# Moving two chunks of weight conversion from the MLP to the experts, and squaring from SBUF instead of PSUM

## The chip, the cores and the metric

The kernel runs on one core of a Trainium2 chip. The metric is the device time of one execution in microseconds (us), here the median of three runs. One more execution was recorded by the profiler; all rows of the trace come from that one.

## The reference

Three stages run one after the other on 3072 tokens of width 256. The first is a chunked linear attention. The second is a mixture of experts in which every token goes to one of eight. The third is an MLP whose hidden layer is squared after the relu:

```python
def _moe_ref(x, w_gate, w1, w2):
    ...
        h = np.maximum(xe @ w1[e], 0.0)
        ye = h @ w2[e]
...
def _moe2_ref(x, w_in, w_out):
    h = x @ w_in              # 256 -> 2048
    r = np.maximum(h, 0.0)
    g = r * r
    return (g @ w_out).astype(np.float32)   # 2048 -> 256
```

## The kernel before, in words

Every float32 product is made from parts that TensorE takes at its fast rate: an operand is split into a high part (rounded to fp32r) and a low part (what is left), and three products are summed (high by high, high by low, low by high).

**Experts** (`Moe.run`). The work is a written-out list of 72 steps: 16 for the most used expert, which is cut into two parts, and eight for each of the other seven, whose columns shrink from 440 to 360. A step n does `up` for one slice of 128 hidden units (six matmuls into one PSUM bank `h`, of which there are two; ScalarE makes the high part `hh`, VectorE the low part `hl`) and then `down` for the slice of two steps earlier (six matmuls). The counter w = n - 8 sets everything else. Expert weights come in four pieces an expert, `wst` (two loads of 256 KB each, L153 and L155, issued by SyncE), with three buffers; piece w//2+7 is loaded in each odd step, ScalarE makes its high part `whi` (L161) four steps after the load was issued, VectorE its low part `wlo` (L168) in two halves.

**Conversion of the MLP's weights** (`Wide`). The MLP's two weight matrices arrive as 64-bit floats in 16 chunks of 512 KB (`wide.load`, L199 and L202, tile `w64`, two buffers). `Wide.step` turns a chunk into a high and a low part in three steps: i=0 is one ScalarE instruction (L222) and three of VectorE (L223 to L225), i=1 one of ScalarE (L228) and two of VectorE (L227, L229), i=2 two of VectorE (L231, L232). Chunks 0 to EARLY_W - 1 are converted inside the experts' steps, from the steps in the list `starts`; a chunk's third step also issues the load of the chunk two further on. The other chunks are converted inside the MLP, three to one step before they are needed (the table `conv` in `Mlp.run`).

**MLP** (`Mlp.run`). Tokens are cut into seven tiles: tile 0 and the last one have 256, the others 512. The steps are again a list: five slices of tile 0 (n = 0 to 4), then in turn one slice of tiles 1, 2 and 0, and from step 48 on one tile after the other. Step n does, in this order on each queue: what `conv` holds for n, then `up`, then the `down` of step n-3. `up` is six matmuls into a bank `h` (L983; three banks), then ScalarE `r` = relu (L987), VectorE `q` = square (L988), ScalarE `ga` = high part (L989), VectorE `gb` = low part (L990). `down` is six matmuls (L1005) for a slice of tile 0 and twelve for one of 512 tokens; the third of them is the first that reads `gb`. Each engine works through its own queue in order, so on ScalarE the `r` of the next step stands behind the `ga` of this one, and on VectorE the next `q` behind this `gb`. A third of the steps (tile 2) also carry one small instruction of a table (`rest_table`). At slice 8 of tiles 2 to 5 the next tile's input is split, its low part by GpSimd (`zl`, L969).

The lines that matter are these:

```python
steps += [(e, 2, f) for e in range(1, NE) for f in range(8)]     # Moe.run
starts = [6 + 52 * c // EARLY_W for c in range(EARLY_W)]
...
if w in (1, 4):
    wide.load(w // 4)
...
nc.scalar.activation(r, ps, ACTF.Relu)                           # Mlp.up
nc.vector.scalar_tensor_tensor(q, ps, 0.0, r, ALU.max, ALU.mult)
nc.scalar.activation(a, q, ACTF.Copy)
nc.vector.tensor_tensor(b, q, a.bitcast(F32), ALU.subtract)
```

Of the kernel before, what the change touches and what calls it, by code (L numbers as in the profile page):

```python
# [16 lines left out]
ALU = mybir.AluOpType  # L17
# [14 lines left out]

FILL = 512

EARLY_W = 10

AHEAD = 5
REG = 3584
# [85 lines left out]
class Ring:  # L124
# [45 lines left out]
    def up(self, part, e, f, kd):  # L170
        t = part[(4 * e + f // 2) % len(part)]
        o = kd * 256 + (f % 2) * 128
        return t[:, o:o + 128]
# [558 lines left out]
class Moe:  # L732
# [153 lines left out]
    def run(self, after):  # L886

        k = self.k
        ring, wide, v = k.ring, k.wide, k.nc.vector
        steps = [(0, 0, f) for f in range(8)] + [(0, 1, f) for f in range(8)]  # L890
        steps += [(e, 2, f) for e in range(1, NE) for f in range(8)]
        starts = [6 + 52 * c // EARLY_W for c in range(EARLY_W)]

        nz = (T - CAP) // 8
        zero = k.pad[:, 0:1].to_broadcast([128, nz])
        self.down(*steps[5])
        self.turn((0, 1), 0, 1)
        self.down(*steps[6])
        self.down(*steps[7])
        for n in range(8, len(steps)):  # L900
            e, part, f = steps[n]
            self.up(e, part, f)
            for j in ([] if n < 10 else [n - 2]):
                self.down(*steps[j])
                pe_, pp, pf = steps[j]
                if pf == 7 and pp:
                    self.store(pe_)
            w = n - 8
            if w < 8:
                c = CAP + w * nz  # L910
                k.nc.scalar.activation(k.z[:, 0, c:c + nz], zero, ACTF.Copy)
                k.nc.vector.memset(k.z[:, 1, c:c + nz], 0.0)
            if f == 0 and 0 < e < NE - 1:
                self.load_rows((e + 1, 2))
            if f == 2 and e + 1 < NE:
                self.note((e + 1, 2))
            if f == 2 and e + 2 < NE:
                self.fill(e + 2)
            ring.low(w // 2 + 4, v, w % 2, 2)
            if w % 2 == 1:  # L920
                ring.high(w // 2 + 5)
                ring.load(w // 2 + 7)
            if w in (1, 4):
                wide.load(w // 4)
            for c, w0 in enumerate(starts):
                if w0 <= w < w0 + 3:
                    wide.step(c, w - w0)
                if w == w0 + 2 and c + 2 < 16:
                    wide.load(c + 2)
            if f in (3, 5) and e + 1 < NE:  # L930
                self.turn((e + 1, 2), f // 4)
            if w == 61:
                after()
        self.down(*steps[-2])
        self.down(*steps[-1])
        self.store(NE - 1)


class Mlp:
# [36 lines left out]
    def up(self, t, m):  # L976
        k, nc, wide = self.k, self.k.nc, self.k.wide
        n = self.COLS[t + 1] - self.COLS[t]
        ps = self.ps_h.tile([128, 512], F32, tag="h", name="h2")[:, 0:n]
        i = 0  # L980
        for kd in range(2):
            for wt, zt in ((wide.ih, self.zh), (wide.il, self.zh), (wide.ih, self.zl)):
                nc.tensor.matmul(ps, wt[:, kd, m * 128:m * 128 + 128], zt[t][:, kd], start=(i == 0), stop=(i == 5))  # L983
                i += 1
        r, q = (self.gp.tile([128, 512], F32, tag=x, name=x)[:, 0:n] for x in ("r", "q"))
        a, b = (self.g2.tile([128, 512], F32R, tag=x, name=x)[:, 0:n] for x in ("ga", "gb"))
        nc.scalar.activation(r, ps, ACTF.Relu)  # L987
        nc.vector.scalar_tensor_tensor(q, ps, 0.0, r, ALU.max, ALU.mult)  # L988
        nc.scalar.activation(a, q, ACTF.Copy)  # L989
        nc.vector.tensor_tensor(b, q, a.bitcast(F32), ALU.subtract)  # L990
        self.gh[t, m], self.gl[t, m] = a, b
# [33 lines left out]
    def run(self):  # L1025
# [26 lines left out]
        conv = {}  # L1052
        for c in range(EARLY_W, 16):
            for i in range(3):
# [237 lines left out]
```

## Time and profile before

| | |
|---|---|
| median of 3 runs | 560.36 us (560.28 to 562.75) |
| profiled execution | 559.56 us |
| its span, first to last instruction | 557.9 us |
| busy TensorE matmul, weight load | 509.4 us (91%), 458.8 us (82%) |
| busy VectorE, ScalarE, GpSimd | 365.0 us (65%), 253.2 us (45%), 105.9 us (19%) |
| mean granted clock of TensorE | 0.968 of full speed |

The attention takes the first 110 us or so, the experts run until 265.5 us, the MLP from there to the end. A busy share says how much of a stretch an engine had an instruction in it; idle time costs something only where another engine, or the end, waits for it. The matmuls' ends are modelled, so their starts are the better guide. A wait for several semaphores is put down to the one that came last by the trace; where that engine had long been done, it was another, often a transfer.

### The profile page before, as it was taken

How to read it: one execution, taken by the hardware profiler on the slowest of the kernel's cores; microseconds unless marked ns; L12 is line 12 of the kernel's file. 1: busy time of each engine (PE TensorE's matmuls, PEld its weight loads, DVE VectorE, ACT ScalarE, POOL GpSimd, SP SyncE). 2: the span in 40 equal slices, each digit the busy share in tenths (PEclk: the TensorE clock that was granted, in tenths of full speed). 3: DMA queues.
4: the chain of work that ended last, by engine and by line, in shares of the span. 5: the costliest groups of instructions: out<-in, count | busy, mean ns of one | idle time of the engine just before them, and what ended most of it. 6: DMA issues, size and time to landing. Idle time of an engine off the chain costs nothing.

```text
span 557.9 us, 11394 instructions
## 1 busy us (share of the span) xinstructions
PE 509.4 (91%) x4293; PEld 458.8 (82%) x4293; DVE 365.0 (65%) x792; ACT 253.2 (45%) x479; POOL 105.9 (19%) x130
## 2 busy tenths in 40 slices
PE   5876987967999999999799999999999999999991
PEld 3654766867899999999688988889999999999991
DVE  8963876637988889893777777665464445444460
ACT  3511113436456566543544444454554554544550
POOL 6754641610110110000000001010510210201201
PEclk9987989879999999999999999999999999999997
DMA  6779746669977886750111100000200100000000
GB/s 203 207 189 264 224 133 173 190 153 265 220 167 223 201 208 214 217 98 0 39 39 38 39 2 1 1 20 1 75 1 2 38 1 1 29 10 1 29 12 21
DMA packets 42714, 55.08 MB, mean 99 GB/s; under 512 B 10400, under 2 KB 30752, under 8 KB 42656
## 3 DMA queue, kind: packets, MB, share of 16 engines
q1 hardware_dynamic: 38912, 43.81, 29.4%
q0 software_dynamic: 3600, 10.05, 6.0%
q8 instruction: 35, 0.57, 0.4%
q10 hardware_dynamic: 144, 0.46, 0.2%
q14 instruction: 23, 0.19, 0.1%
HBM read 43.96 MB, written 10.33 MB: 97 GB/s over the span
## 4 chain that ended last, share of the span: by engine, by line
PE 55%; DVE 16%; DMA 10%; issue 8%; ACT 5%; POOL 3%; SPq 1%; POOLq 0%; ACTq 0%; DVEq 0%
PE u L1005 16%; PE h L983 15%; PE h L839 8%; PE o L855 7%; DVE q L988 4%; DMA wst<-in_w_dram 3%; ACT ga L989 3%; DVE gb L990 2%; PE y L447 2%; PE y L454 2%; DMA mc<-pad 1%; PE dS L418 1%; PE tp L467 1%; DVE wlo L168 1%; DMA CT<-in_ct_dram 1%
## 5 line engine op out<-in xcount | busy, mean ns | idle before, releaser
L990 DVE TENSOR_TENSOR gb<-q,ga 128x512 fp32r<-128x512 f32 (+1 forms) x112 | 69.1, 617 | 71.4 <-ACT ga L989 67.8
L989 ACT ACTIVATE ga<-q 128x512 fp32r<-128x512 f32 (+1 forms) x112 | 63.9, 571 | 104.4 <-DVE q L988 104.4
L1005 PE MATMUL u<-woh,ga 128*128 128x256 f32 x384 | 108.2, 282 | 0.6 <-ACT ob L1017 0.6
L1005 PE MATMUL u<-wol,ga 128*128 128x256 f32 x384 | 108.1, 281 | 0.0
L1005 PE MATMUL u<-woh,gb 128*128 128x256 f32 x384 | 107.2, 279 | 0.0
L988 DVE SCALAR_TENSOR_TENSOR q<-h,r 128x512 f32<-128x512 f32 (+1 forms) x112 | 68.5, 612 | 38.7 <-ACT r L987 37.9
L983 PE MATMUL h<-zh,wih 128*128 128x512 f32 (+1 forms) x224 | 82.7, 369 | 6.7 <-DVE q L988 6.7
L983 PE MATMUL h<-zh,wil 128*128 128x512 f32 (+1 forms) x224 | 80.8, 361 | 0.0
L983 PE MATMUL h<-zl,wih 128*128 128x512 f32 (+1 forms) x224 | 80.7, 360 | 0.0
L1005 PEld LDWEIGHTS u<-woh,ga 128*128 128x128 f32 x384 | 72.1, 188 | 4.3 <-ACT ob L1017 0.8
L1005 PEld LDWEIGHTS u<-wol,ga 128*128 128x128 f32 x384 | 72.1, 188 | 3.2
L987 ACT ACTIVATE r<-h 128x512 f32<-128x512 f32 (+1 forms) x112 | 59.3, 529 | 34.0 <-PE h L983 33.2
L1005 PEld LDWEIGHTS u<-woh,gb 128*128 128x128 f32 x384 | 72.5, 189 | 0.1
L842 ACT ACTIVATE hh<-h 128x256 fp32r<-128x256 f32 (+8 forms) x72 | 33.8, 471 | 55.3 <-PE h L839 53.0
L844 DVE SCALAR_TENSOR_TENSOR hl<-h,hh 128x256 fp32r<-128x256 f32 (+8 forms) x72 | 38.1, 529 | 24.7 <-ACT hh L842 24.7
L983 PEld LDWEIGHTS h<-zh,wih 128*128 128x128 f32 x224 | 42.1, 188 | 13.0 <-DVE q L988 9.5
L1018 POOL DMA_INDIRECT out_dram<-ob,idx x24 | 23.9, 997 | 132.7 <-ACT ob L1017 127.0
L855 PE MATMUL o<-hh,whi 128*128 128x256 f32 (+8 forms) x144 | 48.4, 336 | 0.0
L855 PE MATMUL o<-hh,wlo 128*128 128x256 f32 (+8 forms) x144 | 48.2, 334 | 0.0
L855 PE MATMUL o<-hl,whi 128*128 128x256 f32 (+8 forms) x144 | 48.1, 334 | 0.0
L983 PEld LDWEIGHTS h<-zl,wih 128*128 128x128 f32 x224 | 42.1, 188 | 7.3
L839 PE MATMUL h<-xh,whi 128*128 128x208 f32 (+7 forms) x128 | 44.9, 351 | 3.3 <-DVE hl L844 3.2
(195 smaller groups left out, 894.9 us busy)
## 6 DMA issues: line engine op xcount, KB each, us to landing
wst<-in_w_dram SPq DMA_DIRECT2D x64, 256.0 KB, 4.2
X<-in_xx_dram SPq DMA_DIRECT2D x48, 128.0 KB, 3.5
w<-in_win_dram SPq DMA_DIRECT2D x8, 512.0 KB, 6.3
w<-in_wout_dram SPq DMA_DIRECT2D x8, 512.0 KB, 3.8
xs<-pad POOLq DMA_DIRECT2D x7, 516.0 KB, 8.1
BB<-in_bb_dram SPq DMA_DIRECT2D x6, 512.0 KB, 4.8
Cb<-in_cc_dram SPq DMA_DIRECT2D x24, 128.0 KB, 4.0
xr<-xs SPq DMA_DIRECT2D x4, 516.0 KB
```

Of the source, the lines that this page charges most:

```text
L447: pe.matmul(y[32 * c:32 * c + 32, hq], M[:, hq, c8, :], X2[p][:, 0, b2, :, c8 * 64 + hq * 32:c8 * 64 + hq * 32 + 32], start=(hq == 0), sto ...
L839: nc.tensor.matmul(ps, ring.up(wt, e, f, kd), xt[:, kd], start=(i == 0), stop=(i == 5))
L842: nc.scalar.activation(a, ps, ACTF.Relu)
L844: rest = lambda: nc.vector.scalar_tensor_tensor(b, ps, 0.0, a.bitcast(F32), ALU.max, ALU.subtract)
L855: nc.tensor.matmul(self.yps[e][d][:, c:c + n], ring.down(wt, e, f, d), ht, start=(f == 0 and i == 0), stop=(f == 7 and i == 2))
L983: nc.tensor.matmul(ps, wt[:, kd, m * 128:m * 128 + 128], zt[t][:, kd], start=(i == 0), stop=(i == 5))
L987: nc.scalar.activation(r, ps, ACTF.Relu)
L988: nc.vector.scalar_tensor_tensor(q, ps, 0.0, r, ALU.max, ALU.mult)
L989: nc.scalar.activation(a, q, ACTF.Copy)
L990: nc.vector.tensor_tensor(b, q, a.bitcast(F32), ALU.subtract)
L1005: nc.tensor.matmul(o, gt[:, q * 128:q * 128 + 128], wt[:, m], start=(m == 0 and i == 0 and h == 0), stop=(m == 15 and i == 2), skip_group_ ...
L1018: ins = nc.gpsimd.indirect_dma_start(out=k.out, out_offset=bass.IndirectOffsetOnAxis(ap=self.idx[:, c:c + 1], axis=0), in_=ob, in_offset=N ...
```

## The change

The MLP's square is made from `r` alone, as `r * r` from SBUF, where it was `max(h, 0) * r` with `h` in PSUM; the bank `h` is then read by ScalarE only. Twelve chunks, not ten, are converted beside the experts. The first starts at step w = 10, not 6, and the starts stand 4 or 5 steps apart (10, 14, 18, 22, 26, 30, 35, 39, 43, 47, 51, 55) where they stood 5 or 6 apart (6, 11, 16, 21, 26, 32, 37, 42, 47, 52). The first two loads of chunks go out at w = 4 and 7, not 1 and 4. The MLP is left with chunks 12 to 15.

```diff
-EARLY_W = 10
+EARLY_W = 12
...
-        starts = [6 + 52 * c // EARLY_W for c in range(EARLY_W)]
+        starts = [10 + 50 * c // EARLY_W for c in range(EARLY_W)]
...
-            if w in (1, 4):
-                wide.load(w // 4)
+            if w in (4, 7):
+                wide.load(w // 7)
...
         nc.scalar.activation(r, ps, ACTF.Relu)
-        nc.vector.scalar_tensor_tensor(q, ps, 0.0, r, ALU.max, ALU.mult)
+        nc.vector.tensor_tensor(q, r, r, ALU.mult)
         nc.scalar.activation(a, q, ACTF.Copy)
```

On SyncE's queue, in steps w = 1 to 4 of the experts, it stood so before (`wst_1434` is the buffer of weight piece 8, which ScalarE reads in step 7; `w_2024` and `w_2140` are chunks 0 and 1):

```order
L155 DMA wst_1433<-in_w_dram 128x2x256
L199 DMA w_2024<-in_win_dram 128x512
L1239 TENSOR_LOAD ord
...
L153 DMA wst_1434<-in_w_dram 128x2x256
L155 ISA
L155 DMA wst_1434<-in_w_dram 128x2x256
L199 DMA w_2140<-in_win_dram 128x512
```

and now, down to step 7 (`w_2138` and `w_2213` are chunks 0 and 1):

```order
L155 DMA wst_1433<-in_w_dram 128x2x256
L1239 TENSOR_LOAD ord
...
L153 DMA wst_1434<-in_w_dram 128x2x256
L155 ISA
L155 DMA wst_1434<-in_w_dram 128x2x256
L199 DMA w_2138<-in_win_dram 128x512
...
L155 DMA wst_1433<-in_w_dram 128x2x256
L199 DMA w_2213<-in_win_dram 128x512
```

Piece 8 had one chunk's load ahead of it and one right behind it; now it has none ahead.

On VectorE's queue, at the start of the MLP (steps n = 0 to 4), it stood so before:

```order
L969 TENSOR_TENSOR zl<-z,zh 128x512 x2
L988 SCALAR_TENSOR_TENSOR q<-h_3957,r 128x256
L990 TENSOR_TENSOR gb<-q,ga 128x256
L223 TENSOR_SCALAR w_3973<-w_3973 128x512
L224 TENSOR_SCALAR w_3972<-w_3973 128x512
L225 SCALAR_TENSOR_TENSOR w_3972<-w_3584,w_3972 128x512
L988 SCALAR_TENSOR_TENSOR q<-h_3978,r 128x256
L990 TENSOR_TENSOR gb<-q,ga 128x256
L227 TENSOR_SCALAR w_3973<-w_3972 128x512
L229 SCALAR_TENSOR_TENSOR w_3973<-w_3584,w_3973 128x512
...
L231 TENSOR_TENSOR w_3972<-w_3972,woh 128x512
L232 TENSOR_TENSOR wol<-w_3972,w_3973 128x512
```

and now:

```order
L969 TENSOR_TENSOR zl<-z,zh 128x512 x2
L988 TENSOR_TENSOR q<-r 128x256
L990 TENSOR_TENSOR gb<-q,ga 128x256
...
L969 TENSOR_TENSOR zl<-z,zh 128x512 x2
L988 TENSOR_TENSOR q<-r 128x256
L990 TENSOR_TENSOR gb<-q,ga 128x256
L988 TENSOR_TENSOR q<-r 128x256
L990 TENSOR_TENSOR gb<-q,ga 128x256
L988 TENSOR_TENSOR q<-r 128x512
L990 TENSOR_TENSOR gb<-q,ga 128x512
```

The seven instructions of chunk 10 are gone from between the squares, and so are those of chunk 11 in steps 7 to 9; the first that still stand there are chunk 12's, in step 13.

## Rows read from the trace of the kernel before

**Rows 1.** Windows: us; busy PE, PEld, DVE, ACT, POOL; PEclk; DMA share; GB/s.

```profile
220.00:240.00 20.00, 20.00 (x118) 19.49 (x117) 17.97 (x34) 12.22 (x21) 2.28 (x3) 1.00 0.71 193
...
360.00:380.00 20.00, 20.00 (x127) 17.93 (x126) 11.80 (x21) 10.44 (x19) 2.08 (x2) 1.00 0.04 14
```

**Rows 2.** Waits of PE: for whom, us in total, times, longest.

```profile
PE h L983 <- DVE q L988: 6.7, 11, 1.6
```

**Rows 3.** Timeline of PE: start, us, instruction, and the idle time before it.

```profile
138.40 0.47 PE L839 MATMUL h<-xh,whi 128*128 128x440 f32 x1 [2.64 <-DVE hl L844]
...
265.53 0.28 PE L983 MATMUL h<-zh,wih 128*128 128x256 f32 x1
...
355.64 0.28 PE L983 MATMUL h<-zh,wih 128*128 128x256 f32 x1
```

**Rows 4.** Chain that ended last, merged, 354 to 359 us: start, us, what.

```profile
354.38 1.42 PE u L1005 x12
355.80 0.70 PE h L983 x6
356.50 0.71 PE u L1005 x6
357.21 1.40 PE h L983 x6
```

**Rows 5.** Timeline of DVE, 262 to 356 us.

```profile
267.66 0.42 DVE L988 SCALAR_TENSOR_TENSOR q<-h,r 128x256 f32<-128x256 f32 x1
...
270.66 0.42 DVE L988 SCALAR_TENSOR_TENSOR q<-h,r 128x256 f32<-128x256 f32 x1
...
272.97 0.42 DVE L988 SCALAR_TENSOR_TENSOR q<-h,r 128x256 f32<-128x256 f32 x1
...
276.93 0.42 DVE L988 SCALAR_TENSOR_TENSOR q<-h,r 128x256 f32<-128x256 f32 x1
...
278.17 0.42 DVE L988 SCALAR_TENSOR_TENSOR q<-h,r 128x256 f32<-128x256 f32 x1
...
279.56 0.69 DVE L988 SCALAR_TENSOR_TENSOR q<-h,r 128x512 f32<-128x512 f32 x1
...
281.56 0.68 DVE L988 SCALAR_TENSOR_TENSOR q<-h,r 128x512 f32<-128x512 f32 x1
...
285.08 0.42 DVE L988 SCALAR_TENSOR_TENSOR q<-h,r 128x256 f32<-128x256 f32 x1
...
287.39 0.68 DVE L988 SCALAR_TENSOR_TENSOR q<-h,r 128x512 f32<-128x512 f32 x1
...
290.71 0.68 DVE L988 SCALAR_TENSOR_TENSOR q<-h,r 128x512 f32<-128x512 f32 x1
...
344.31 1.40 DVE L224 TENSOR_SCALAR w<-w 128x512 int32<-128x512 int32 x1
...
353.35 0.69 DVE L990 TENSOR_TENSOR gb<-q,ga 128x512 fp32r<-128x512 f32 x1 [0.70 <-ACT ga L989]
```

**Rows 6.** Timeline of ACT, one instruction of step w = 7 of the experts.

```profile
135.70 1.06 ACT L161 ACTIVATE whi<-wst 128x1024 fp32r<-128x1024 f32 x1 [3.86 <-PE o L855]
```

**Rows 7.** Timeline of SyncE's queue: two loads at the start of the experts.

```profile
124.05 0.47 SPq L199 DMA_DIRECT2D w<-in_win_dram  x1
...
126.56 0.37 SPq L155 DMA_DIRECT2D wst<-in_w_dram  x1
```

**Rows 8.** Loads of `wst`, issue to landing: those issued 125.8 to 127 us, 140 to 250 us.

```profile
DMA to landing us min/median/max: 9.0/9.2/9.5
...
DMA to landing us min/median/max: 2.7/4.0/7.6
```

**Rows 9.** Groups by line and form: busy us, mean ns.

```profile
L988 DVE SCALAR_TENSOR_TENSOR q<-h,r 128x512 f32<-128x512 f32 x80 | 55.1, 689 | 36.3 <-ACT r L987 35.9
...
L224 DVE TENSOR_SCALAR w<-w 128x512 int32<-128x512 int32 x16 | 7.8, 488 | 0.5
```

**Rows 10.** Line L990 from 355 us: ns min/median/max, first and last start.

```profile
L990 DVE TENSOR_TENSOR gb<-q,ga x78: 424/692/764, 355.2 to 544.7; 128x512 fp32r<-128x512 f32 x60, 128x256 fp32r<-128x256 f32 x18
```

## The prediction

> **What bounds the kernel now.** I read the windows first. At 220 to 240 us and again at 360 to 380 us TensorE has a matmul in it all the time, at granted clock 1.00, the upper of its two levels; only faster matmuls could shorten such a stretch, and the change touches none [rows 1]. So the time to be won is where TensorE waits. The waits of TensorE name one large item outside the attention: the MLP's `up` on VectorE's `q`, 6.7 us [rows 2]. The timeline of TensorE shows a single long one in the experts, 2.64 us at 138.40 us [rows 3].
>
> How much the MLP loses is seen better from starts than from idle time. Step 0's `up` starts at 265.53 us, step 37's at 355.64 us: 90.1 us [rows 3]. The work between is 15 `up` of 256 tokens, 22 of 512, 14 `down` of 256 and 20 of 512. Their prices stand in the chain, where TensorE is dense: 0.70, 1.40, 0.71 and 1.42 us [rows 4]. That makes 10.5 + 30.8 + 9.9 + 28.4 = 79.6 us. TensorE loses 10.5 us there, more than the waits say.
>
> The timeline of VectorE tells why. From one `q` to the next it takes 1.24 us after a 256-token step (276.93 to 278.17), 1.39 us from a 256 to a 512 one, 2.00 us after a 512 one (279.56 to 281.56) [rows 5]. Only about two thirds of that is work: `gb` waits 0.70 us for ScalarE's `ga`, which waits for `q` [rows 5]. Three steps, 512, 512 and 256, thus take VectorE 2.00 + 2.00 + 1.24 = 5.2 us, and TensorE 7.0 us by its prices. A conversion put between them is added in full, because the queue is in order. So in the steps that hold conversions the chain VectorE to ScalarE to VectorE is the bound.
>
> **The change, part by part.**
>
> *Chunks 10 and 11 leave the MLP.* Chunk 10 stretched the step 267.66 to 270.66 to 3.00 us instead of 1.24, and 270.66 to 272.97 to 2.31 instead of 1.24; chunk 11 stretched 281.56 to 285.08 to 3.52 instead of 2.00, 285.08 to 287.39 to 2.31 instead of 1.39, and 287.39 to 290.71 to 3.32 instead of 2.00 [rows 5]. That is 1.76 + 1.07 and 1.52 + 0.92 + 1.32. Chunk 10's last part lies beside another instruction (272.97 to 276.93 also holds a tile's split), so I price it like chunk 11's, 1.32. Together 7.9 us come off the chain. Would TensorE become late instead? Before step 12 stand seven `up` of 256 and five of 512, six `down` of 256 and three of 512: 4.9 + 7.0 + 4.3 + 4.3 = 20.4 us by prices. TensorE starts step 12 at 285.9 us, ends its `up` at 287.3 and has `r`, which I put at 0.7 us like a VectorE instruction of its size, at 288.0. The chain has step 9's `q` 7.9 us before 290.71, at 282.8, and step 12's 2.00 + 1.39 + 2.00 later, at 288.2 [rows 5]. They nearly meet, so all 7.9 us count, and from chunk 12 on the chain bounds as before. Step 33's `gb`, which now ends at 353.35 + 0.69 = 354.0 us [rows 5], then ends at 346.1; ten of the twelve matmuls of its `down` follow (1.2 us) [rows 4], and step 37 starts at 347.3 us instead of 355.64: **8.3 us**. Bounds: at most the whole loss of 10.5 us; at least about 7, if TensorE is a us later at step 12 than its prices say. After step 37 TensorE is full again [rows 1] and keeps what it has won.
>
> *The square from SBUF.* The instruction costs the same: 689 ns with one input in PSUM, and 692 for `gb`, which has both in SBUF [rows 9, 10]. Its gain is that a bank is free after `r`, not after `q`. But the `down` behind that `up` waits for `gb`, later in the same chain. With the old square step 36 would start at the end of step 33's `q` (353.35 - 0.70 - 7.9 = 344.8) and step 37 at 344.8 + 1.40 + 1.42 = 347.6 us, 0.3 later [rows 4, 5]. So this edit is worth 0.3 us of the 8.3, and nothing where no conversions are.
>
> *The first chunk loads go out three steps later.* The stall at 138.40 goes back to ScalarE, which could make the high part of weight piece 8 only at 135.70 us; the row names a matmul, but the piece's second load, issued at 126.56, landed 9.0 us later, at 135.6, behind a chunk's 512 KB from 124.05 [rows 6 to 8]. It has no chunk ahead of it now. A landing of 9.0 - 2.64 = 6.4 us would cost nothing; the median later is 4.0; only at 9 or more is nothing won [rows 3, 8]. Chunk 0's instructions go from steps 6 to 8 too. I take **2.6 us**, bounds 0 and 3.
>
> *Two more chunks in the experts.* A chunk is 1.52 + 1.07 + 1.32 = 3.9 us of VectorE's queue, two 7.8 us, which is the worst case. VectorE is busy 17.97 of 20 us beside the experts [rows 1]; from 140 to 250 us that leaves some 11 us idle. The 7.8 us fit, but in the later experts, whose steps are shorter, nothing is left over, and with starts 4 apart a queue late by two us holds a bank. I take a loss of **0.5 us**, bounds 0 and 7.8. ScalarE gets four instructions more at 12.22 of 20 us [rows 1]; SyncE issues two more loads of 512 KB there and two fewer in the MLP; GpSimd's queue is unchanged.
>
> **The sum.** 8.3 + 2.6 - 0.5 = 10.4 us off the profiled execution's 559.56 us, or 549.2; that execution lies 0.8 us under the median of the runs, so the median should be **550.0 us**.
>
> **The rivals.**
>
> *The early stall stays* (the load is late for another reason, such as GpSimd's own transfers): 552.6 us. For it: 9 us is far from the median. Against: the one thing ahead of it on its queue is moved away.
>
> *The conversions carry their price along.* If VectorE is the bound of the experts from the first chunk on, the 7.8 us are lost there instead of 0.5: 557.3 us; a third of it gives 552. For it: 17.97 of 20 us, and single queues in order. Against: TensorE is full in that window, so the present load does not hold it up.
>
> *The square is held up by GpSimd.* `q` now takes both inputs from SBUF as GpSimd's `zl` does. A conversion instruction at 344.31 took 1.40 us instead of a mean 0.49 while GpSimd split a tile [rows 5, 9], so such holding exists. Against: `gb`, with two inputs in SBUF, took 764 ns at most beside such splits, 0.07 over its median [rows 10]. If a square is held like that conversion, 0.9 us each, in the two halves of the one split that falls into the bound stretch, the time is 551.8 us. The Trainium skill (SBUF — State Buffer, "Who interferes with whom") says that a VectorE instruction with two SBUF inputs contends with a GpSimd instruction that reads SBUF, and that the second to issue blocks fully. By that rule this edit is a loss; the maximum for `gb` does not agree with a full block.
>
> *Slower than before: weight pieces late all through the experts.* A piece is used four steps after it was issued. A step has twelve matmuls, and 118 take 20 us, so that is some 8 us [rows 1]; a landing over that stalls TensorE, as at 138.40 for 2.64 us. Eleven chunk loads now go out while pieces are loaded, closer together. If five of them do what one does now, 13.2 us are lost: 563.2 us; four are the break-even. Against: from 140 to 250 us, with nine chunk loads, no landing exceeded 7.6 us, median 4.0 [rows 8].
>
> *The change does nothing*, because the chain in the MLP is slow for a reason other than the conversions: 560 us. The stretched intervals speak against it.
>
> **How the numbers follow.** Forecast, within 547 and 551.4: 0.52. Early stall stays: 0.17. Conversions carry some of their price (552 to 557.3): 0.14. Held square: 0.06. Better than 547, if the chain leaves less of the 10.5 us: 0.04. No change: 0.04. Slower: 0.03. A measurement of this kernel can tell about 0.5%, 2.8 us, from no change. Below 557.6 lie all but the last two: faster 0.93, same 0.04, slower 0.03. The range 547 to 554 us leaves out what is better than 547, the dearer half of the conversions' case, no change and slower, some 0.18.
>
> **What would show it.** Right: no wait of TensorE near 135 to 139 us; steps 0 to 12 of the MLP without a gap over 0.5 us; from step 0's `up` to step 37's some 82 us where it was 90.1; the remaining loss near steps 33 to 37, at `down` and no longer at `up`; `q` at 0.69 us. Wrong: waits of `up` (L839) on `hl` between 190 and 250 us, or VectorE never idle there; `whi` waiting for `wst`; `q` over 0.75 us; a first half that ends no earlier than 265 us.

## The result, and the profile after

The changed kernel took 554.38 us (median of 6 runs, 550.43 to 555.19) where the kernel before took 561.17 in the same comparison: a ratio of 0.987, 95% interval 0.983 to 0.991. It was timed twice more as an experiment and gave 0.991 (0.988 to 0.994) and 0.990 (0.985 to 0.995). So it is about 1.1% faster, some 6 us of 560, where 10.4 us were forecast. The ratios, here and below, are formed from the fast runs of both kernels and are not quotients of the medians. The profiled execution took 554.26 us, span 552.6 us.

I divide the work by five starts of TensorE's `up`: `w` = 0, S0 (`w` = 8, the first step of expert 1), S8 (`w` = 16, the first step of expert 2), M0 (step 0 of the MLP) and M37 (step 37 of the MLP). Experts are counted from 0, the most used one; the second expert is expert 2, the sixth is expert 6. The timeline of TensorE after, the answer to [rows 3], has these starts, and the stalls between:

```profile
118.77 0.36 PE L839 MATMUL h<-xh,whi 128*128 128x208 f32 x1
...
131.66 0.38 PE L839 MATMUL h<-xh,whi 128*128 128x440 f32 x1
...
142.03 0.70 PE L820 MATMUL tpm<-cst,xr 128*128 128x128 f32 x4 [1.64 <-DMA xr<-xs]
...
154.64 0.35 PE L839 MATMUL h<-xh,whi 128*128 128x424 f32 x1
...
235.96 0.44 PE L839 MATMUL h<-xh,whi 128*128 128x376 f32 x1 [1.59 <-DVE hl L844]
...
267.92 0.28 PE L983 MATMUL h<-zh,wih 128*128 128x256 f32 x1
...
350.35 0.28 PE L983 MATMUL h<-zh,wih 128*128 128x256 f32 x1
```

| stretch | before | after | difference |
|---|---|---|---|
| `w` = 0 to S0 | 12.11 | 12.89 | +0.78 |
| S0 to S8 | 23.19 | 22.98 | -0.21 |
| S8 to M0 | 111.10 | 113.28 | +2.18 |
| M0 to M37 | 90.11 | 82.43 | -7.68 |

The starts before are these; M0 and M37 are in [rows 3]:

```profile
119.13 0.38 PE L839 MATMUL h<-xh,whi 128*128 128x208 f32 x1
...
131.24 0.38 PE L839 MATMUL h<-xh,whi 128*128 128x440 f32 x1
...
154.43 0.35 PE L839 MATMUL h<-xh,whi 128*128 128x424 f32 x1
```

The MLP did nearly what was forecast. The waits of TensorE in the MLP, 268 to 360 us, were 6.7 us for `q` [rows 2]; now they are, in the same columns:

```profile
PE u L1005 <- DVE gb L990: 0.5, 2, 0.2
PE u L1005 <- ACT ga L989: 0.4, 1, 0.4
```

From M37 on nothing changed: M37 comes 5.29 us earlier and the span is 5.3 us shorter. What is missing in this profile was lost in the experts. The stall of 2.64 us at 138.40 [rows 3] is gone, but another of 1.64 us stands 3.6 us later, for the rows of the next expert, and one of 1.59 us is new at 235.96. The windows of the profile after show what followed the first of them, TensorE's granted clock at its lower level (1.2 of 2.4 GHz) for three microseconds (columns as in [rows 1]):

```profile
142.00:143.00 1.00, 0.97 (x5) 0.78 (x6) 1.00 (x2) 0.86 (x2) 0.47 (x1) 0.94 0.60 203
143.00:146.00 3.00, 3.00 (x10) 2.68 (x9) 1.98 (x5) 0.83 (x2) 1.04 (x2) 0.50 0.61 85
146.00:148.00 2.00, 2.00 (x11) 1.88 (x10) 1.97 (x4) 0.00 (x0) 0.00 (x0) 0.93 0.55 87
```

The stall at 235.96 is read from two engines. First the timeline of ScalarE, then that of VectorE:

```profile
232.19 1.06 ACT L161 ACTIVATE whi<-wst 128x1024 fp32r<-128x1024 f32 x1 [2.84 <-DMA wst<-in_w_dram]
233.15 0.64 ACT L222 ACTIVATE w<-w 128x512 f32<-128x512 f32 x1
233.70 0.47 ACT L842 ACTIVATE hh<-h 128x376 fp32r<-128x376 f32 x1
```

```profile
233.82 0.43 DVE L223 TENSOR_SCALAR w<-w 128x512 f32<-128x512 f32 x1 [2.27 <-ACT w L222]
234.29 0.43 DVE L224 TENSOR_SCALAR w<-w 128x512 int32<-128x512 int32 x1
234.75 0.69 DVE L225 SCALAR_TENSOR_TENSOR w<-w,w 128x512 int32<-128x512 int32 x1
235.36 0.54 DVE L844 SCALAR_TENSOR_TENSOR hl<-h,hh 128x376 fp32r<-128x376 f32 x1
```

A weight piece is late by 2.84 us, so ScalarE makes its high part (L161) late. Behind it in the queue stands the first instruction of a chunk's conversion (L222). VectorE has nothing ready but that conversion's L223 and sits idle for 2.27 us, then runs L223, L224 and L225, and only then `hl`, which `up` waits for. The question for the runs was which half of this is the cause: the late piece, or the conversion in the two queues.

### The profile page after: what moved, and what is told of

The parts are those of the page before. It is cut to its first block, busy times and chain, and to the rows that moved or that the text cites. A ratio compares the mean times of both kernels' runs of the same rounds, so it can differ in the third digit from the quotient of the medians.

```text
span 552.6 us, 11396 instructions
## 1 busy us (share of the span) xinstructions
PE 507.0 (92%) x4293; PEld 458.7 (83%) x4293; DVE 368.1 (67%) x792; ACT 252.7 (46%) x479; POOL 107.7 (19%) x130
## 4 chain that ended last, share of the span: by engine, by line
PE 64%; DVE 12%; DMA 10%; issue 6%; POOL 3%; ACT 2%; SPq 0%; DVEq 0%; POOLq 0%; ACTq 0%
PE u L1005 22%; PE h L983 21%; PE h L839 8%; PE o L855 8%; DMA wst<-in_w_dram 4%; DVE wlo L168 2%; DMA mc<-pad 2%; DMA xr<-xs 1%; DMA xs<-row,ixi 1%; DVE hl L844 1%; DMA CT<-in_ct_dram 1%; DVE st L435 1%; PE y L447 1%; PE y L454 1%; POOL Qm L383 1%
## 5 line engine op out<-in xcount | busy, mean ns | idle before, releaser
L990 DVE TENSOR_TENSOR gb<-q,ga 128x512 fp32r<-128x512 f32 (+1 forms) x112 | 69.7, 622 | 71.3 <-ACT ga L989 67.0
L988 DVE TENSOR_TENSOR q<-r 128x512 f32<-128x512 f32 (+1 forms) x112 | 69.3, 619 | 37.5 <-ACT r L987 36.4
L983 PE MATMUL h<-zh,wih 128*128 128x512 f32 (+1 forms) x224 | 81.1, 362 | 0.0
L842 ACT ACTIVATE hh<-h 128x256 fp32r<-128x256 f32 (+8 forms) x72 | 33.8, 470 | 53.1 <-PE h L839 52.7
L983 PEld LDWEIGHTS h<-zh,wil 128*128 128x128 f32 x224 | 42.0, 187 | 3.8
```

The costliest lines, as they stand in the source:

```text
L842: nc.scalar.activation(a, ps, ACTF.Relu)
L988: nc.vector.tensor_tensor(q, r, r, ALU.mult)
```

## The experiments

In what follows, T1 is the theory that the loss in the experts is late transfers, T2 that it is more work than the queues of VectorE and ScalarE hold. All kernels of one group ran on one chip and are compared with the kernel before on that chip (559.55, 568.75 and 560.08 us; the groups are rows 1 to 4, 5 to 8 and 9 to 12 of the table).

| kernel | median us | ratio to before (95%) | S0 to S8 | S8 to M0 | M0 to M37 |
|---|---|---|---|---|---|
| square alone | 557.13 | 0.9985 (0.995 to 1.002) | 20.86 | 112.13 | 89.92 |
| old square | 553.06 | 0.9885 (0.9835 to 0.9935) | 22.39 | 113.33 | 82.88 |
| second load at step 9 | 551.41 | 0.9861 (0.9812 to 0.991) | 23.35 | 111.88 | 82.45 |
| no chunk loads | 550.30 | 0.9849 (0.9803 to 0.9896) | 21.22 | 111.42 | 82.43 |
| every fourth step | 559.56 | 0.9849 (0.9801 to 0.9897) | 19.62 | 109.94 | 82.43 |
| eleven chunks | 562.25 | 0.9913 (0.9881 to 0.9945) | 19.77 | 110.08 | 85.81 |
| late start alone | 568.67 | 0.9987 (0.995 to 1.0023) | 22.03 | 111.32 | 90.13 |
| changed, second time | 563.05 | 0.991 (0.9877 to 0.9943) | 23.24 | 110.87 | 82.45 |
| changed, third time | 553.13 | 0.9898 (0.985 to 0.9947) | 22.42 | 112.20 | 82.42 |
| every fourth step, again | 549.31 | 0.982 (0.9776 to 0.9865) | 21.05 | 109.94 | 82.44 |
| thirteen chunks | 549.40 | 0.9812 (0.9767 to 0.9857) | 23.45 | 109.95 | 81.76 |
| loads without work | 551.47 | 0.9842 (0.9794 to 0.989) | 23.44 | 109.94 | 82.42 |

The last three columns are differences of starts in one profile each, as above.

### The square alone, and everything but the square

The kernel before with one line changed:

```diff
-        nc.vector.scalar_tensor_tensor(q, ps, 0.0, r, ALU.max, ALU.mult)
+        nc.vector.tensor_tensor(q, r, r, ALU.mult)
```

> The kernel before with only the square taken from SBUF. If the gain of the changed kernel comes from the two conversions that leave the MLP (the prediction), this alone gives 0.3 us: step 0's up to step 37's up stays at 89 to 90 us (90.1 before), the whole at 559 to 560.5 us beside the kernel before. If instead the shared bank was the brake (rival), the waits of up for q go here too, that stretch falls by 3 us or more, to 87 or less, and the whole gets faster by 3 us or more.

The changed kernel with that line put back:

> The changed kernel with the square read from PSUM again, so the moved conversions and loads alone. Prediction: 0.3 us slower than the changed kernel, up0 to up37 82.5 to 83 us (82.4 in the changed kernel), and about 6 us faster than the kernel before. Rival (shared bank the brake): waits of up for q come back, up0 to up37 at 85 us or more, and the gain over the kernel before falls to 3 us or less.

The square is worth 0.19 us in the MLP of the kernel before (90.11 to 89.92) and 0.45 in that of the changed one (82.88 to 82.43); the other 7.2 to 7.5 us are the two conversions. By the time, the square alone cannot be told from nothing. What it does is change the name of the wait, not its cause. TensorE's waits from 268 to 360 us with the square alone:

```profile
PE u L1005 <- ACT ga L989: 2.8, 3, 1.1
PE u L1005 <- DVE gb L990: 1.6, 7, 0.2
```

and in the changed kernel with the old square:

```profile
PE h L983 <- DVE q L988: 2.1, 4, 0.9
```

With the square alone `up` waits for `q` no longer, but `down` then waits for `ga` and `gb` of the same chain, and the stretch is as long as it was. The shared bank was not the brake.

### The second load behind the rows

```diff
-            if w in (4, 7):
-                wide.load(w // 7)
+            if w in (4, 9):
+                wide.load(w // 9)
```

> The changed kernel with the second chunk's load at step 9 instead of 7, so that it stands behind the rows of the second expert in SyncE's queue. Theory T1 (a 512 KB chunk load ahead of the rows of the next expert makes these late, and the stall takes TensorE's clock down): the 1.6 us wait of the transposes for xr near 142 us goes, and with it the four microseconds at a granted clock of 0.50 behind it; the experts gain 1.6 to 3.2 us and the whole is 551 to 553 us. Rival T2 (the place of the load is nothing; VectorE and ScalarE have too much in their queues): the stall stays within 0.5 us and the whole is 554 us.

The wait for `xr` is gone, and yet S0 to S8 took 23.35 us: another stall, of 1.86 us for `hl`, stands at 136.25 us, and behind it the granted clock is at its lower level again (0.50 from 137 to 139 us). This was a hit by the letter of T1 (no wait for `xr`, 551.41 us) and not in its substance, for the time was not won there. The later profiles took the letter too: with the load at step 9, "every fourth step, again" waits 1.25 us for `xr` after all (below), and the changed kernel's third profile, with the load at step 7, does not wait for it.

### No chunk loads, and loads without work

Chunks 2 to 11 converted from the data of chunks 0 and 1, without loads of their own:

```diff
+        if 2 <= n < EARLY_W:
+            self.st[n] = self.src[n % 2]
+            return
         st = self.tmp.tile([128, 512], I64, tag="w64", name="w64")
+        if n < 2:
+            self.src[n] = st
```

> The changed kernel with all twelve conversions kept but only chunks 0 and 1 loaded for them: chunks 2 to 11 are converted again from the data of the first two, so the weights of the MLP are not the reference's. Ten loads of 512 KB are left out of the experts, the work on VectorE and ScalarE is the same. T1 (late transfers are the whole loss of the experts): the 1.6 us stall near 236 us and the 0.23 us ones behind it go, whi is not kept waiting for wst there; the experts from 150 us on end about 2.1 us earlier than in the changed kernel, the whole is 551 to 552.5 us (the early stall near 142 us stays, since its load stays). T2 (denser conversions in the in-order queues): the stalls near 236 us stay at 1 us or more, the whole is 554 us.

And the reverse, all loads in their places and almost no arithmetic:

```diff
+        if 2 <= n < EARLY_W:
+            if i == 1:
+                s.activation(oh, hi.bitcast(F32), ACTF.Copy)
+            if i == 2:
+                v.tensor_copy(ol, hi.bitcast(F32))
+                self.t.pop(n)
+                self.st.pop(n)
+            return
```

> The changed kernel with all its loads, but without the conversion's arithmetic for chunks 2 to 11: one copy on ScalarE and one on VectorE stand for seven instructions, so the weights of the MLP are not the reference's. T1 (loads): the experts lose as much as in the changed kernel, the wait for xr at the second expert stays, step 8 to the MLP 111 to 113.3 us, the whole within 1 us of the changed kernel. T2 (work in the queues of VectorE and ScalarE): no stall, step 8 to the MLP at 110 us or below, the whole 2 to 4 us faster than the changed kernel.

Neither theory stands alone. Without loads there is no stall over 0.5 us after S8, as T1 says, but S8 to M0 is 111.42 us, and `whi` waits 0.96 us for its piece even so. Without work it is 109.94, as T2 says, as short as in any profile; the whole is 1.7 us under the changed kernel of its group, between what the two had. The loads-without-work profile has the piece late all the same. Its ScalarE, then its VectorE (eight lines were added ahead, so `hh` is L850 and `hl` L852):

```profile
233.93 1.06 ACT L161 ACTIVATE whi<-wst 128x1024 fp32r<-128x1024 f32 x1 [2.35 <-DMA wst<-in_w_dram]
234.90 0.47 ACT L850 ACTIVATE hh<-h 128x376 fp32r<-128x376 f32 x1
```

```profile
235.39 0.55 DVE L852 SCALAR_TENSOR_TENSOR hl<-h,hh 128x376 fp32r<-128x376 f32 x1 [2.63 <-ACT hh L850]
```

From the late L161 to `hl` are 235.39 - 233.93 = 1.46 us here and 235.36 - 232.19 = 3.17 in the changed kernel. The difference, 1.7 us, is the conversion's first step between them, and it is about the difference between no stall of TensorE and one of 1.59 us.

### Conversions at every fourth step

From the 12 starts 10 + 50c/12 (10, 14, 18, 22, 26, 30, 35, 39, 43, 47, 51, 55), which from the seventh on are odd steps, to even steps throughout:

```diff
-        starts = [10 + 50 * c // EARLY_W for c in range(EARLY_W)]
+        starts = [10 + 4 * c for c in range(EARLY_W)]
...
-            if w in (4, 7):
-                wide.load(w // 7)
+            if w in (4, 9):
+                wide.load(w // 9)
```

> The changed kernel with the conversions begun at every fourth step exactly (10, 14, ... 54), so that every chunk is loaded at the first or the fifth step of an expert, and none at its second, one step ahead of the fill of a later expert's rows, as at 219.5 us in the changed kernel; and with the second load at step 9. Same twelve conversions, same work on VectorE and ScalarE. T1 (which load meets which): whi near 230 us waits for its piece by less than 1.5 us (2.8 in the changed kernel, 2.9 with the old square), no stall over 0.5 us after 150 us, none for xr near 142 us; step 8 to the MLP 111 to 112 us (113.3 in the changed kernel); the whole 549 to 552 us. T2 (too much work in the queues of VectorE and ScalarE): a stall of over 1 us stays in the fifth or sixth expert, 554 us.

> Every fourth step and the second load at step 9, once more and beside the changed kernel. T1: no wait for xr at the second expert, no stall over 0.5 us from step 8 on, step 8 to the MLP at 110 us, the whole 2 to 4 us faster than the changed kernel of the same chip (0.985 of the kernel before). Rival: the 3.5 us of the earlier pair was scatter; the two are within 1 us.

The high part of a weight piece is made in odd steps (`ring.high`, where `w % 2 == 1`), and in program order just ahead of a conversion that begins in that step. With even starts the conversion's first instruction stands behind `hh`, in another step than the piece. ScalarE in "every fourth step, again":

```profile
223.15 1.06 ACT L161 ACTIVATE whi<-wst 128x1024 fp32r<-128x1024 f32 x1 [0.32 <-PE o L855]
...
224.72 0.49 ACT L842 ACTIVATE hh<-h 128x384 fp32r<-128x384 f32 x1
225.11 0.67 ACT L222 ACTIVATE w<-w 128x512 f32<-128x512 f32 x1
```

S8 to M0 was 109.94 us in both profiles (109.95 with thirteen chunks, 110.08 with eleven), with no wait of TensorE over 0.2 us in it. TensorE is busy all of that time, so no wait is left there to be won ("every fourth step, again", columns as in [rows 1]):

```profile
152.74:262.68 109.94, 109.94 (x623) 108.10 (x622) 97.80 (x182) 62.59 (x108) 6.88 (x9) 1.00 0.68 184
```

In both profiles the piece at about 230 us was in time as well, so these two runs do not part the order of the steps from the timing of the loads; "eleven chunks", with the same even starts, has that piece 1.18 us late and still takes 110.08. The whole was 3.5 us faster than the changed kernel of the same chip (559.56 to 563.05) and 3.8 us in the second pair (549.31 to 553.13), where the two kernels' runs do not overlap: 548.74 to 551.55 against 552.45 to 557.26. In the second pair that settles it against scatter; in the first the runs overlap. Of it 0.9 and 2.3 us lie between S8 and M0 in the profiles; the rest is before S8 (S0 to S8 took 19.62 against 23.24 and 21.05 against 22.42), which differs from profile to profile, and whether the second load at step 9 has a part in it stays open. One clause of T1 missed in the second profile, the wait for `xr` (TensorE's timeline):

```profile
141.68 0.70 PE L820 MATMUL tpm<-cst,xr 128*128 128x128 f32 x4 [1.25 <-DMA xr<-xs]
...
152.74 0.35 PE L839 MATMUL h<-xh,whi 128*128 128x424 f32 x1
...
262.68 0.28 PE L983 MATMUL h<-zh,wih 128*128 128x256 f32 x1
```

### The changed kernel again, twice

Without an edit.

> The changed kernel once more, for a second profile and beside the others on one chip. If the experts' loss of 2.4 us is fixed by the order of the loads, the stall of 1.6 us near 236 us is here again (it was 1.7 us with the old square); the stall between 131 and 154 us may lie elsewhere, since it differed in every profile so far. The whole 552 to 555 us.

> The changed kernel a third time, as the yardstick of the three beside it. So far it was 0.987 and 0.991 of the kernel before. Expected 0.986 to 0.992; the transposes wait 0.3 to 1.9 us for xr at the second expert (five of five profiles with the second load at step 7 so far did, none of three with it at step 9), and the stall of 1.6 us in the sixth expert may be there or not (in two of three profiles with these starts and all loads at 4 and 7, with either square).

The stall of the sixth expert is not fixed by the order of the instructions: none in the second profile (where no piece was late there), 0.56 us in the third. Put beside each other, all profiles with the starts 10 + 50c/12 line up by how long `whi` waited for its piece at about 230 us (ScalarE's timeline):

| profile | `whi` waits | S8 to M0 | over 109.94 |
|---|---|---|---|
| changed, second time | 0 | 110.87 | 0.93 |
| no chunk loads | 0.96 | 111.42 | 1.48 |
| second load at step 9 | 1.43 | 111.88 | 1.94 |
| changed, third time | 1.81 | 112.20 | 2.26 |
| changed kernel | 2.84 | 113.28 | 3.34 |
| old square | 2.91 | 113.33 | 3.39 |
| loads without work | 2.35 | 109.94 | 0.00 |
| eleven chunks, even starts | 1.18 | 110.08 | 0.14 |

In the one profile where no piece was late, the odd starts cost 0.93 us by themselves. Beyond the first half microsecond, each one by which the piece is then late costs another; with the conversion at even steps, or none, it costs next to nothing. So what is lost beyond 0.93 us takes both: a late piece, and a conversion begun right behind it. Set step by step against "every fourth step, again", the starts at 35, 39 and 43 cost about 0.1 us together and those at 47 and 55 some 0.35 and 0.5, in the late experts whose steps are shortest; the late piece, made in step 47, adds 0.36, 0.72, 1.76 and 1.84 us in step 50 (second load at step 9, changed third, changed, old square), its lateness less about 1.1 us, and every profile with the late piece loses 0.5 more in step 52. The late start alone begins no conversion at step 47: its piece there is 2.10 us late, and no stall for `hl` follows.

### The late start alone

The kernel before (ten chunks, old square) with:

```diff
-        starts = [6 + 52 * c // EARLY_W for c in range(EARLY_W)]
+        starts = [10 + 50 * c // EARLY_W for c in range(EARLY_W)]
...
-            if w in (1, 4):
-                wide.load(w // 4)
+            if w in (4, 7):
+                wide.load(w // 7)
```

> The kernel before with the later loads and later start alone: first two chunks loaded at steps 4 and 7, conversions from step 10, ten chunks beside the experts, square from PSUM. Prediction (term A): 2.6 us (0 to 3) faster than the kernel before, because the wait of 2.64 us at 138 us goes. Rival: the stall of 138 us comes and goes from one execution to the next (0.35 us there in the kernel with the square alone, with the same loads), and the late loads only move it to the rows of the second expert: 0 us within the measurement, with one stall of 1 to 3 us between 131 and 154 us in the profile; that stretch takes 22 to 23.5 us (23.2 before, 20.9 with the square alone).

0.9987 (0.995 to 1.0023), 0.1 us by the medians: this part of the change cannot be told from nothing, though the interval just reaches the 2.6 us of the prediction. The stall moved; TensorE and, in the changed kernel's third profile, TensorE and ScalarE:

```profile
145.14 0.47 PE L839 MATMUL h<-xh,whi 128*128 128x440 f32 x1 [1.58 <-DVE hl L844]
```

```profile
138.19 0.47 PE L839 MATMUL h<-xh,whi 128*128 128x440 f32 x1 [2.46 <-DVE hl L844]
```

```profile
136.01 1.06 ACT L161 ACTIVATE whi<-wst 128x1024 fp32r<-128x1024 f32 x1 [4.07 <-DMA wst<-in_w_dram]
```

In that third profile the piece is 4.07 us late with the chunk loads at steps 4 and 7, and TensorE's stall is the old one almost to the place. S0 to S8 took 19.6 to 23.5 us over fourteen profiles, and no place of the loads stands out: 20.9 and 23.2 us with loads at steps 1 and 4 (square alone, before), 21.2 to 23.4 at 4 and 7, 19.6 to 23.5 at 4 and 9. The loads up to step 7 go out before S0, so the whole stretch from `w` = 0 to S8 counts too: 33.8 and 35.3 us, 33.7 to 36.2, and 32.7 to 36.4, in the same order. The windows show why moving one load might not help: from 131 to 142 us the DMA engines are full, in the kernel before, the changed one and its third profile:

```profile
131.00:142.00 11.00, 8.00 (x46) 7.15 (x45) 8.64 (x18) 5.21 (x10) 0.07 (x1) 1.00 1.03 296
```

```profile
131.00:142.00 11.00, 9.39 (x56) 8.59 (x55) 7.98 (x18) 6.71 (x11) 0.00 (x0) 1.00 0.95 310
```

```profile
131.00:142.00 11.00, 7.81 (x43) 7.25 (x44) 7.15 (x16) 5.33 (x10) 0.00 (x0) 1.00 1.04 332
```

At a share of 0.95 to 1.04 some transfer is the last, whichever goes first. That is an argument from these rows, not a run: a kernel without the first two chunk loads in that stretch was not tried, and what decides which transfer is late in an execution stays open.

### Eleven and thirteen chunks

Both with even starts and the second load at step 9, and `EARLY_W = 11` or `EARLY_W = 13`.

> The same order of loads with eleven chunks beside the experts, the twelfth again in the MLP. Prediction's sum: each chunk that leaves the MLP is worth about half of 7.7 us, so the MLP's stretch (step 0's up to step 37's up) is 86 us (90.1 before, 82.4 in the changed kernel) and the whole 3 to 4 us above that with twelve. Rival: one chunk already takes the MLP off the conversions' chain, so the stretch is below 84 us and the whole within 1 us of that with twelve.

> The same order with thirteen chunks beside the experts, the last begun at step 58. The MLP of the changed kernel waits only 0.4 and twice 0.2 us for ScalarE and VectorE, and TensorE is the rest: a thirteenth chunk that leaves it is worth 0 to 1 us there (81.5 to 82.4 us), and within 1 us in the whole, of the run with twelve. Rival (the chain of conversions still sets the MLP's pace): 3.5 to 4 us faster, as the twelfth chunk was (85.8 with eleven, 82.4 with twelve).

From the square alone (ten chunks, 89.92 us) the eleventh chunk takes the MLP to 85.81, the twelfth to 82.43, the thirteenth to 81.76: 4.1, 3.4 and 0.7 us. The chain of conversions is the bound up to twelve, and then TensorE is: with thirteen it is busy 81.09 of the 81.76 us. The whole with eleven is 2.7 us over the one with twelve (562.25 to 559.56), a little under the 3 to 4 expected; with thirteen it is that with twelve (549.40 and 549.31). Every fourth step with twelve or thirteen chunks is the version to keep: 0.981 to 0.985 of the kernel before, and 3.5 to 3.8 us under the change as made, measured with twelve.

## Why the prediction was right, and where it was not

**What bounds the MLP: right.** The loss was the chain from VectorE to ScalarE and back, lengthened by conversions in an in-order queue, and it left with them: 82.43 us, where some 82 were named as the sign, and 82.42 to 82.88 in all nine profiles with twelve chunks.

**Chunks 10 and 11, with the square: right, 0.6 us too high.** 8.3 us were forecast, from 90.1 to 81.8; it was 7.68. Bounds of 7 to 10.5 held it. By its stretched intervals chunk 10 was worth 1.76 + 1.07 + 1.32 = 4.15 us and chunk 11 3.76; they measured 4.1 and 3.4. The waits left are at `down`, near the end of the stretch, as forecast, 0.9 us together.

**The square: right in its worth, not in its duration.** 0.3 us forecast, 0.19 and 0.45 measured. But `q` does not always take 0.69 us now. VectorE in the changed kernel, and GpSimd's splits beside it:

```profile
409.89 1.00 DVE L990 TENSOR_TENSOR gb<-q,ga 128x512 fp32r<-128x512 f32 x1 [0.70 <-ACT ga L989]
...
453.12 0.89 DVE L988 TENSOR_TENSOR q<-r 128x512 f32<-128x512 f32 x1 [0.83 <-ACT r L987]
...
454.71 1.02 DVE L990 TENSOR_TENSOR gb<-q,ga 128x512 fp32r<-128x512 f32 x1 [0.70 <-ACT ga L989]
...
497.92 1.12 DVE L988 TENSOR_TENSOR q<-r 128x512 f32<-128x512 f32 x1 [0.72 <-ACT r L987]
```

```profile
407.27 3.08 POOL L969 TENSOR_TENSOR zl<-z,zh 128x512 fp32r<-128x512 f32 x2 [10.77 <-ACT zh L968]
...
452.17 3.01 POOL L969 TENSOR_TENSOR zl<-z,zh 128x512 fp32r<-128x512 f32 x2 [14.46 <-ACT zh L968]
...
496.87 1.62 POOL L969 TENSOR_TENSOR zl<-z,zh 128x256 fp32r<-128x256 f32 x2 [14.25 <-ACT zh L968]
```

Two of the 80 squares of 512 tokens took 0.89 and 1.12 us, and each of these long instructions starts while a split of GpSimd runs. With the square from PSUM no square exceeded 0.69 us, and one `gb` took 0.76. The rival of the held square thus named a real thing, at 0.2 to 0.4 us a piece and not 0.9; all four lie behind M37, where TensorE has work in hand, and cost nothing. The Trainium skill (SBUF — State Buffer, "Who interferes with whom") has the contention of a VectorE instruction with two SBUF inputs, and these rows bear that out. It calls the shared pair of ports an exclusive lock and speaks of a full block in its lines on the two-port modes, which the prediction took over for two inputs; these rows do not decide that. The four start some 0.5 us before the end of a split (of its half, where two run on end, taken as equal) and grow by 0.20 to 0.43 us, and a square of 0.68 us at 408.52 did not grow though a split ran beside it.

**The first loads three steps later: wrong, and it is the larger part of what is missing.** The step that failed: "It has no chunk ahead of it now", and from it "I take **2.6 us**". Alone it measured 0.1 us, with an interval from 2.8 us won to 1.3 lost. The stall of 138.40 us was read as an outcome of one load standing ahead of another, from one execution. The square alone, with the loads unchanged, had 0.35 us in that place, and the third profile of the changed kernel had 2.46 with the loads moved. A stall that comes and goes between executions is no term of a sum. The rival "the early stall stays", 552.6 us, is what happened in effect, and stood at 0.17.

**Two more chunks in the experts: the size not told from the forecast, the reason incomplete.** 0.5 us were taken, with bounds of 0 and 7.8. Against the kernel before's 111.10 us from S8 to M0, three profiles of the changed kernel lose 2.2 and 1.1 us and win 0.2. But that is one profile of the kernel before: the square alone, whose experts are the same, took 112.13 there, with waits of 0.82 and 0.75 us for `xr`, and the old square, whose experts are the changed ones, 113.33. By these two and four profiles the loss is 0.8 us (112.4 against 111.6), less than they scatter. The reason given was VectorE's time ("The 7.8 us fit, but in the later experts ... nothing is left over"). The time does fit there too: at every fourth step the same twelve conversions take S8 to M0 to 109.94, under the kernel before. What the prediction did not look at is on which steps the conversions begin and what stands ahead of them on ScalarE. The rival of late pieces had half of it, and expected it at five places for 2.64 us each; it came at one.

**The signs.** Of those named for being right, the 82 us and the waits left at `down` came, and no wait near 135 to 139 us in the first profile, though one of 2.46 us in the third. Of those named for being wrong, four came: `up` waited 1.59 us on `hl` at 235.96 us, `whi` 2.84 us for `wst`, two squares took over 0.75 us, and the first half ended at 267.92 us, not before 265.

**The sum.** 7.7 us in the MLP, less 0.8 between S8 and M0 and 1.1 between `w` = 0 and S8 (35.7 us in the mean of the same four profiles against 34.5 in the two), is 5.8 us, where the three comparisons say 0.987 to 0.991, or 5.0 to 7.3 us of 560. How that loss is shared between the two stretches is not settled by so few profiles. The range on record, 547 to 554 us, was stated for a kernel before at 560.36 us; 0.987 of that is 553.1, inside it, but above the 547 to 551.4 us that were thought most likely. That it lies inside is owed to the width of the range, which took in two of the rivals; the sum itself came out 3 us too low, most of it by the term of the first loads.

## What to carry to other kernels

Before a stall in one profile becomes a term of a sum, look at whether the runs of that kernel scatter by as much as the stall; where its cause was a transfer in a stretch with the DMA engines full, moving one load here only moved the stall. When work is spread through an in-order queue, the idle share says only whether it fits; which instruction of another engine its first step waits for says what it costs, so begin it on steps where nothing that can be late stands ahead of it.

## What was not expected of the hardware

- After some stalls of TensorE its granted clock was at the lower level for some 3 to 4 us, after others it was not, and the stall's length does not sort them: 0.50 after a wait of 1.64 us in the changed kernel (above), 0.58 from 148 to 151.5 us after 1.89 us in its second profile, but 1.00 after 2.46 us in its third and after the 2.64 us at 138.40 in the kernel before. The rows of the second and the third:

```profile
148.00:151.50 3.50, 3.50 (x13) 3.03 (x12) 2.49 (x5) 1.41 (x3) 1.50 (x2) 0.58 0.63 134
```

```profile
138.00:142.00 4.00, 3.81 (x19) 3.58 (x20) 3.97 (x9) 2.40 (x4) 0.00 (x0) 1.00 1.00 341
```

  What tells the two apart was not settled; three to four microseconds at half the clock cost an estimated 1.5 to 2 us, so it makes the price of a stall uncertain by about the stall itself.
- The three groups' kernel before took 559.55, 568.75 and 560.08 us, and the middle group ran on another chip than the other two: 9 us, more than all that is studied here. Whole times were compared on one chip only.
